# Attention with a capacity-gated expert layer: one expert's second layer kept back until the attention's last block

## The chip, the core and the metric

The kernel runs on one core of a Trainium2 chip. The metric is the time of one execution in device microseconds (us), the median of several runs. TensorE (PE in the rows) does the matmuls, VectorE (DVE), ScalarE (ACT) and GpSimd (POOL) the elementwise work, and SyncE (SP) issues most of the DMAs. Each engine works through its own list of instructions in order.

## What is computed

Attention with capped scores over 8 batches of 12 heads, 448 positions of 64 elements; then, in each batch, the 128 rows with the highest gate score go through a two-layer expert, and the result is added to them.

```python
scores = cap * np.tanh(scale * np.matmul(q, k.transpose(0, 1, 3, 2)) / cap)
attn = np.exp(scores - np.max(scores, axis=-1, keepdims=True))
attn = attn / (np.sum(attn, axis=-1, keepdims=True) + 1e-09)
x = np.matmul(attn, v)                     # -> (8, 448, 768)
gate = np.einsum('bsd,d->bs', x, w_gate)
out = x.copy()
for b in range(B):
    top_idx = np.argpartition(-gate[b], capacity)[:capacity]   # capacity 128
    xe = x[b, top_idx]
    ye = np.maximum(xe @ w1, 0.0) @ w2      # 768 -> 1024 -> 768
    g = 1.0 / (1.0 + np.exp(-gate[b, top_idx]))
    out[b, top_idx] = x[b, top_idx] + g[:, None] * ye
```

## The kernel before

Twelve heads make three groups of four, so there are 24 "doubles" (8 batches x 3 groups), numbered 0 to 23; doubles 18 to 20 are batch 6, 21 to 23 batch 7. A double takes seven steps; a step makes one 128 x 896 tile `p` (or `pl`, for the last 64 keys of two pairs): eight score matmuls (L225) into a PSUM tile `ps`, a tanh (L241) and an exp (L242) on ACT, then four value matmuls (L262, or L258 for `pl`) into the accumulators `x` and `y`. The main loop in `fast_path` takes two steps a turn: TensorE gets the scores of block u and behind them the values of block u-1, whose exps ran meanwhile. There are 84 blocks, u = 0 to 83; in turn 84 only the last values are left, and with u = 85 the loop knows the attention to be over (`u > nblocks`).

VectorE adds the tiles `p` into `e` (L277, L279) and GpSimd adds `pl` to it (L283). `sums_mm` multiplies `e` by ones (L291) for the softmax sums: two matmuls on the `e` of the first pair, two on that of the second. The sums are copied to `sm` (L294), turned (L319) and inverted into `rec` (L322, L325). The accumulators are copied to `xT` (L270), turned (L334) and multiplied by `rec` into `xn` (L338), which is stored to `out`; L351 forms its part of the gate scores.

After a batch's third double its selection runs: the scores are turned into a row (L378, L381), ranked by comparisons (L386, L393, L405), and made a one-hot matrix `sel` (L421), which a matmul turns into row numbers and gate scores (L430; `idx` L440, `gt` L444, L445). An exp on ACT makes the gate (L448). An indirect DMA of GpSimd gathers the rows `xe` (L441); six transposes (L472) and a split into two parts on ACT (`xh`, L474) and DVE (`xl`, L475) prepare them.

The expert (`expert_gen`) has a first layer of two halves of 18 matmuls (L505), each followed by a relu into `hs` (L511) and, some turns later, by four transposes (L472) and a split into `hh` and `hl`. The second layer is two halves `hf` of 24 matmuls each (L525), in two blocks of twelve; then L532 adds the gated result to `xe`, and after the second half an indirect DMA scatters the rows (L535).

`Filler` places selection and expert between the attention's work. `select` moves every selection on; `expert` takes matmuls of the expert at the head of its list, up to `BUDGET` a turn. A generator that yields `STEP` ends the turn for the experts: those behind it wait too. `K.open` allows two selected batches at a time between L430 and the end of their experts. PSUM tiles outside the attention come from two banks, `pt` and `ph`; after the attention four more are given out (`pv`, `ps`). The order on PE, ACT, DVE and POOL is the order in which this code issues; each turn first does what the turn before had deferred, and DVE's list "dve2" comes behind the turn's own `e` and `xT`.

Of the kernel before, what the change touches and what calls it, by code (L numbers as in the profile page):

```python
# [28 lines left out]
class Bank:  # L29


    def __init__(self, pool, tag, acc, wide=False):
        self.pool, self.tag, self.acc, self.wide = pool, tag, acc, wide
        self.free, self.held = (0, 0), False
# [7 lines left out]
class Ctx:  # L42

    def __init__(self):
        self.immediate = True
        self.queues = {"act": [], "dve": [], "dve2": []}
        self.t, self.epoch = 0, 1
        self.want = False
        self.tail = False
        self.x_busy = False  # L50
        self.open = 0
        self.turns = []
# [186 lines left out]
def exp_step(tc, K, D, h, c, ps):  # L239
    p = p_tile(K, D, h, c)  # L240
    tc.nc.scalar.activation(p, ps[:, :, :K.S], AF.Tanh, scale=K.sc)  # L241
    tc.nc.scalar.activation(p, p, AF.Exp, scale=K.cap)  # L242
# [225 lines left out]
def split_part(tc, K, src, hi, lo, i0, w, M):  # L468
    nc = tc.nc
    pt = K.tile_t(500, SPLIT).rearrange("p (i m) -> p i m", m=P)  # L470
    for i in range(w):
        nc.tensor.transpose(pt[:, i, :M], src[:M, (i0 + i) * P:(i0 + i + 1) * P],  # L472
                            K.ident[:M, :M])
    K.defer("act", lambda: nc.scalar.copy(hi[:, i0:i0 + w, :M], pt[:, :w, :M]))  # L474
    K.defer("dve2", lambda: nc.vector.tensor_tensor(  # L475
        lo[:, i0:i0 + w, :M], pt[:, :w, :M], hi[:, i0:i0 + w, :M].bitcast(F32),
        op=ALU.subtract))


STEP = -1  # L480


def expert_gen(tc, K, b, M, idx, gt, xe, xh, xl):
    nc = tc.nc
    S, DM, ND, NF, F = K.S, K.DM, K.ND, K.NF, K.F
    HH = DM // 2

    hs = K.hs
    hh = K.work.tile([P, NF, P], F32R, tag="mh", name="hh", bufs=1)
    hl = K.work.tile([P, NF, P], F32R, tag="ml", name="hl", bufs=1)  # L490
    turned = {}

    def turn(hf):
        split_part(tc, K, hs, hh, hl, 4 * hf, 4, M)
        turned[hf] = K.due(SPLIT)

    def first(hf):
        fs = slice(hf * 512, hf * 512 + 512)
        while not (bank := K.hold()):
            yield STEP  # L500
        ph = bank.tile()
        ops = [(xh, "w1h", i) for i in range(ND)]
        ops += [(xh, "w1l", i) for i in range(ND)] + [(xl, "w1h", i) for i in range(ND)]
        for n, (l, r, i) in enumerate(ops):
            nc.tensor.matmul(ph[:M], lhsT=l[:, i, :M], rhs=K.wts[r][:, i, fs], start=(n == 0),  # L505
                             stop=(n == len(ops) - 1))
            K.t += 233
            yield 233
        K.release(bank)
        K.want = hf == 0  # L510
        K.defer("act", lambda: nc.scalar.activation(hs[:M, fs], ph[:M], AF.Relu))  # L511
        K.turns.append((K.due(EVAC), lambda: turn(hf)))

    def wait_turn(hf):
        if K.immediate and K.turns:
            K.turns.pop(0)[1]()
        while not K.immediate and (hf not in turned or not K.past(turned[hf])):
            yield STEP

    def second(py, hf, blk, start, stop):  # L520
        ds_ = slice(hf * HH, (hf + 1) * HH)
        ops = [(hh, "w2h", i) for i in blk] + [(hh, "w2l", i) for i in blk]
        ops += [(hl, "w2h", i) for i in blk]
        for n, (l, r, i) in enumerate(ops):
            nc.tensor.matmul(py[:M, :HH], lhsT=l[:, i, :M], rhs=K.wts[r][:, i, ds_],  # L525
                             start=(start and n == 0), stop=(stop and n == len(ops) - 1))
            K.t += 176
            yield 176

    def combine(py, hf):  # L530
        ds_ = slice(hf * HH, (hf + 1) * HH)
        nc.vector.scalar_tensor_tensor(out=xe[:M, ds_], in0=py[:M, :HH], scalar=gt[:M],  # L532
                                       in1=xe[:M, ds_], op0=ALU.mult, op1=ALU.add)
        if hf:
            nc.gpsimd.indirect_dma_start(  # L535
                out=K.out[:(b + 1) * S, :],
                out_offset=bass.IndirectOffsetOnAxis(ap=idx[:M, :1], axis=0),
                in_=xe[:M], in_offset=None)

    lo_blk, hi_blk = range(4), range(4, NF)  # L540
    yield from first(0)
    yield from first(1)
    K.x_busy = False
    yield from wait_turn(0)
    for hf in range(2):
        while not (bank := K.hold()):
            yield STEP
        py = bank.tile()
        yield from second(py, hf, lo_blk, True, False)
        if hf == 0:  # L550
            yield from wait_turn(1)
        yield from second(py, hf, hi_blk, False, True)
        K.release(bank)
        K.want = hf == 0
        K.defer("dve", lambda py=py, hf=hf: combine(py, hf))
    K.open -= 1
# [82 lines left out]
def fast_path(tc, K, first, wgen):  # L639
    ND2 = K.B * K.NG  # L640
    Ds = {0: first}
    steps = [(d, h, c) for d in range(ND2) for h, c in ORDERS[d % 2]]
    sums = []
    fill = Filler()

    def at(n):
        if not 0 <= n < len(steps):
            return None
        d, h, c = steps[n]
        return Ds[d], h, c  # L650

    def flush(*names):
        q = K.take()
        for nm in names:
            for f in q[nm]:
                f()

    def turn():
        while K.turns and K.past(K.turns[0][0]) and K.t_ready():
            K.turns.pop(0)[1]()  # L660

    Ds[1] = Double(K, 1)
    Ds[1].load_qk(tc, K, 0)
    Ds[1].load_qk(tc, K, 1)
    Ds[1].load_v(tc, K)
    warm = K.banks[1].tile()
    for _ in range(WARM):
        tc.nc.tensor.matmul(warm[:, :P], lhsT=K.ident, rhs=K.ident, start=True, stop=True)
    load_consts(tc, K)
    K.immediate = False  # L670
    nblocks = len(steps) // 2
    u = 0
    while u <= nblocks or sums or fill.busy() or any(K.queues.values()):
        if u > nblocks and not sums and not K.tail:
            K.start_tail()
        q = K.take()
        for f in q["dve"] + q["act"]:
            f()
        old = [at(2 * u - 2), at(2 * u - 1)]
        new = [at(2 * u), at(2 * u + 1)]  # L680
        ps = [qk_step(tc, K, *s) for s in new if s]
        for s in old:
            if s:
                pv_step(tc, K, *s)
        for n in range(2):
            if new[n]:
                exp_step(tc, K, *new[n], ps[n])
        for s in old:
            if s:
                e_step(tc, K, *s)  # L690
                take_x(tc, K, *s)
        for f in q["dve2"]:
            f()
        for n in (2 * u, 2 * u + 1):
            if n < len(steps):
                d, i = divmod(n, 7)
                with tc.high_priority(offset=HP):
                    if i == 0 and 0 < d < ND2 - 1:
                        Ds[d + 1].load_qk(tc, K, 1)
                    if i == 2 and d + 2 < ND2:  # L700
                        Ds[d + 2] = Double(K, d + 2)
                        Ds[d + 2].load_v(tc, K)
                    if i == 4 and d + 2 < ND2:
                        Ds[d + 2].load_qk(tc, K, 0)
        if not K.tail:
            if sums:
                D = sums.pop(0)
                fill.sel.append(double_gen(tc, K, D, sums_mm(tc, K, D), fill.exp.append))
                if K.C > P and D.grp == K.NG - 1:
                    flush("dve", "act", "dve2")  # L710
                    fill.drain(K)
                    K.immediate = False
            turn()
            fill.select()
            fill.expert(BUDGET)
            flush("dve", "act", "dve2")
            for s in old:
                if s and s[1:] == (1, 2):
                    sums.append(s[0])
            turn()  # L720
            fill.select()
            if not new[0]:
                K.t += TAIL
        else:
            end = K.t + TAIL
            fill.expert(TAIL)
            K.t = max(K.t, end)
            flush("dve", "act", "dve2")
            turn()
            fill.select()  # L730
        next(wgen, None)
        u += 1
# [84 lines left out]
```

## Time and profile before

| | |
|---|---|
| time, median of three runs | 554.97 us (554.33 to 555.19) |
| the profiled execution, its own time | 556.0 us |
| its span, first to last instruction | 554.2 us |
| PE busy | 513.5 us (93%) |
| ACT, DVE, POOL busy | 360.4, 352.2, 139.2 us |
| mean granted TensorE clock | 0.988 of full |

Times below are counted from the span's start. An engine's idle time in front of an instruction is written [idle <-releaser], the releaser being what ended it; a PE instruction's own duration holds some pipeline time, so what a group costs on PE is read from its start to the next one's start. The rows are of the one profiled execution; batch 5's second layer runs from 461.9 to 485.0 us, the attention's last exp ends at 494.33, and the last matmul at 547.9.

### The profile page before, as it was taken

To read this page: it belongs to the slowest core of one execution; us is meant where nothing else is said; L and a number is where in the kernel's file an instruction comes from. 1 tells how busy PE (TensorE), PEld (TensorE's weight loads), DVE (VectorE), ACT (ScalarE), POOL (GpSimd) and SP (SyncE) were. 2 spreads that over 40 slices of the span, in tenths; PEclk is the share of its full clock that TensorE was granted. 3 is DMA by queue.
4 is the path that set the end of the run, shared out by engine and by line. 5 is a ranking of instruction groups with operands and counts; after the bars stand their busy time and mean duration, and the time that the engine had idled before them with its cause. 6 is when DMAs were issued, how large, how long until landed. Compare 5 with 4: busy or idle time off the path is not lost.

```text
span 554.2 us, 8869 instructions
## 1 busy us (share of the span) xinstructions
PE 513.5 (93%) x3446; PEld 260.4 (47%) x3446; DVE 352.2 (64%) x775; ACT 360.4 (65%) x394; POOL 139.2 (25%) x88
## 2 busy tenths in 40 slices
PE   5889989999999999999899998999999998988994
PEld 2223323354544445444454455545454454626884
DVE  1799999757636557665865565854865644865611
ACT  4987976976667574876657775686666866560110
POOL 1565532413212130431122311231313221130000
PEclk9998999999999999999999999999999999998898
DMA  7546653423214231632232331432323412212100
GB/s 256 190 156 190 193 163 119 125 86 101 74 55 149 81 100 39 186 101 84 82 108 85 114 118 34 127 130 67 99 85 107 135 47 87 67 57 69 29 30 34
DMA packets 32034, 57.63 MB, mean 104 GB/s; under 512 B 2944, under 2 KB 25984, under 8 KB 31984
## 3 DMA queue, kind: packets, MB, share of 16 engines
q1 hardware_dynamic: 30704, 50.69, 29.6%
q0 software_dynamic: 1280, 6.29, 3.4%
q8 instruction: 29, 0.48, 0.4%
q14 instruction: 21, 0.17, 0.1%
HBM read 42.81 MB, written 14.16 MB: 103 GB/s over the span
## 4 chain that ended last, share of the span: by engine, by line
PE 69%; DVE 17%; issue 5%; ACT 3%; DMA 2%; POOL 1%; POOLq 0%; DVEq 0%; SPq 0%
PE ps L225 20%; PE ph L525 9%; PE y L262 8%; PE ph L505 8%; PE x L262 8%; DVE jk L351 4%; PE pt L334 3%; PE x L258 3%; PE pt L291 3%; DVE jk L393 2%; DVE e L277 2%; DVE e L279 2%; DVE xT L270 2%; ACT p L241 2%; PE pt L472 2%
## 5 line engine op out<-in xcount | busy, mean ns | idle before, releaser
L241 ACT ACTIVATE p<-ps,sc 128x896 f32<-128x896 f32 x144 | 143.4, 996 | 73.2 <-PE ps L225 61.2
L283 POOL TENSOR_TENSOR e<-e,pl 64x896 f32<-64x896 f32 x48 | 100.5, 2093 | 288.5 <-DVE e L279 235.1
L225 PE MATMUL ps<-q,k 64*64 64x448 f32 x1344 | 150.8, 555 | 6.3 <-DMA k<-in_k 3.5
L242 ACT ACTIVATE p<-p,capc 128x896 f32<-128x896 f32 x144 | 150.2, 1043 | 4.7
L225 PEld LDWEIGHTS ps<-q,k 64*64 64x64 f32 x1344 | 43.5, 133 | 71.0 <-issue 45.8
L262 PE MATMUL y<-p,v 128*64 128x448 f32 x288 | 64.9, 556 | 0.1
L262 PE MATMUL x<-p,v 128*64 128x448 f32 x288 | 64.9, 558 | 0.0
L277 DVE TENSOR_TENSOR e<-p 128x896 f32<-128x896 f32 x48 | 59.8, 1246 | 6.6 <-ACT p L242 6.6
L279 DVE TENSOR_TENSOR e<-e,p 128x896 f32<-128x896 f32 x48 | 53.3, 1111 | 5.4 <-ACT p L242 3.8
L351 DVE CUSTOM_DVE_ANT_0 jk<-xn,wg 112x256 bf16<-112x256 f32 x96 | 51.2, 534 | 2.9
L338 DVE TENSOR_TENSOR xn<-pt,rec 112x512 f32<-112x512 f32 x39 | 26.9, 690 | 26.8 <-PE pt L334 26.2
L241 ACT ACTIVATE pl<-ps,sc 128x896 f32<-128x896 f32 x24 | 24.1, 1003 | 29.1 <-PE ps L225 28.7
L270 DVE COPY xT<-x 128x448 f32<-128x448 f32 x24 | 15.0, 623 | 39.6 <-PE x L262 25.3
L262 PEld LDWEIGHTS x<-p,v 128*64 128x64 f32 x288 | 17.7, 138 | 43.4 <-issue 31.6
L262 PEld LDWEIGHTS y<-p,v 128*64 128x64 f32 x288 | 16.3, 135 | 44.8 <-issue 31.9
L525 PE MATMUL ph<-w2h,hh 128*128 128x384 f32 x112 | 27.6, 359 | 0.0
L242 ACT ACTIVATE pl<-pl,capc 128x896 f32<-128x896 f32 x24 | 25.0, 1042 | 0.8
L505 PE MATMUL ph<-w1l,xh 128*128 128x512 f32 x84 | 25.1, 409 | 0.0
L334 PE MATMUL pt<-ident,xT 128*112 128x128 f32 x156 | 24.4, 279 | 0.7 <-DVE rec L322 0.7
L511 ACT ACTIVATE hs<-ph 128x512 f32<-128x512 f32 x14 | 8.4, 598 | 25.5 <-PE ph L505 25.3
L525 PE MATMUL ph<-w2l,hh 128*128 128x384 f32 x112 | 24.9, 345 | 0.0
L525 PE MATMUL ph<-w2h,hl 128*128 128x384 f32 x112 | 24.9, 345 | 0.0
(143 smaller groups left out, 622.6 us busy)
## 6 DMA issues: line engine op xcount, KB each, us to landing
q<-in_q SPq DMA_DIRECT2D x48, 224.0 KB, 2.6
k<-in_k SPq DMA_DIRECT2D x48, 224.0 KB, 3.2
v<-in_v SPq DMA_DIRECT2D x24, 448.0 KB, 4.1
out<-xn SPq DMA_DIRECT2D x24, 448.0 KB, 3.7
stage<-in_moe_w SPq DMA_DIRECT2D x4, 512.0 KB, 6.0
stage<-in_moe_w SPq DMA_DIRECT2D x5, 384.0 KB, 3.3
hs<-in_moe_w SPq DMA_DIRECT2D x3, 384.0 KB, 3.0
hs<-in_moe_w SPq DMA_DIRECT2D x2, 512.0 KB, 5.5
```

The costliest lines, as they stand in the source:

```text
L225: tc.nc.tensor.matmul(ps[HALF[r], j, :K.S], lhsT=kk, rhs=qq, start=True, stop=True)
L241: tc.nc.scalar.activation(p, ps[:, :, :K.S], AF.Tanh, scale=K.sc)
L242: tc.nc.scalar.activation(p, p, AF.Exp, scale=K.cap)
L262: nc.tensor.matmul(D.acc[h][HALF[j], :K.S], lhsT=D.v[:, (h * 2 + j) * 3 + c, :], rhs=p[:, j, :], start=start, stop=stop)
L277: nc.vector.tensor_tensor(D.E[h], D.P[h, 0], D.P[h, 1], op=ALU.add)
L279: nc.vector.tensor_tensor(D.E[h], D.E[h], D.P[h, 2], op=ALU.add)
L283: nc.gpsimd.tensor_tensor(e[HALF[i]], e[HALF[i]], pl[HALF[i]], op=ALU.add)
L334: nc.tensor.transpose(px[:CP, c * P:(c + 1) * P], D.xT[pair][:, c * CP:(c + 1) * CP], K.ident)
L338: nc.vector.tensor_tensor(xn[:, :, pair * P:(pair + 1) * P].rearrange("p c (h d) -> p c h d", d=K.D), px[:CP].rearrange("p (c h d) -> p c ...
L351: nc.vector.tensor_tensor_reduce(out=jk[:, :W], in0=xn[:, c, :], in1=K.wg[:, grp * W:(grp + 1) * W], scale=1.0, scalar=0.0, op0=ALU.mult, ...
L505: nc.tensor.matmul(ph[:M], lhsT=l[:, i, :M], rhs=K.wts[r][:, i, fs], start=(n == 0), stop=(n == len(ops) - 1))
L525: nc.tensor.matmul(py[:M, :HH], lhsT=l[:, i, :M], rhs=K.wts[r][:, i, ds_], start=(start and n == 0), stop=(stop and n == len(ops) - 1))
```

## The change

A flag `K.drained` is set at the top of each turn: true once all blocks of the attention have been issued. Batch 5's expert (`b == K.B - 3`), once its first layer is out and the first half of `hs` is turned, yields `STEP` until the flag is true. Its 48 matmuls L525, two L532 and its scatter L535 so move behind the attention's last values; they stay ahead of batch 6's expert, which waits in the same list. Nothing is added or dropped.

```diff
-        self.want = False
+        self.want = self.drained = False
...
     yield from first(1)
     K.x_busy = False
     yield from wait_turn(0)
+    while b == K.B - 3 and not (K.drained or K.immediate):
+        yield STEP
     for hf in range(2):
...
     while u <= nblocks or sums or fill.busy() or any(K.queues.values()):
-        if u > nblocks and not sums and not K.tail:
+        K.drained = u > nblocks
+        if K.drained and not sums and not K.tail:
             K.start_tail()
```

TensorE where the second layer of batch 5 began, before: the sums of double 21 (L291), then the held matmuls between the attention's, beside batch 6's selection (`score`, L378).

```order
L291 MATMUL pt<-e,ones 32x448 x4
L525 MATMUL ph<-w2h,hh 128x384 x4
L525 MATMUL ph<-w2l,hh 128x384 x4
L525 MATMUL ph<-w2h,hl 128x384 x4
L472 MATMUL pt<-ident,hs 128x128 x4
L225 MATMUL ps<-q,k 64x448 x8
L258 MATMUL x<-pl,v 64x448 x2
L258 MATMUL y<-pl,v 64x448 x2
L262 MATMUL x<-p,v 64x448 x2
L378 MATMUL pt<-ident,score 112x112 x4
```

The same place on TensorE now, a block and a half long.

```order
L291 MATMUL pt<-e,ones 32x448 x4
L472 MATMUL ph<-ident,hs 128x128 x4
L225 MATMUL ps<-q,k 64x448 x8
L258 MATMUL x<-pl,v 64x448 x2
L258 MATMUL y<-pl,v 64x448 x2
L262 MATMUL x<-p,v 64x448 x2
L378 MATMUL pt<-ident,score 112x112 x4
L319 MATMUL ph<-ident,sm 112x128 x4
L225 MATMUL ps<-q,k 64x448 x8
L262 MATMUL y<-p,v 64x448 x4
L334 MATMUL pt<-ident,xT 112x128 x4
```

The L525 are gone from there, and the transposes of `hs` go to bank `ph`, so that L378 no longer takes the bank that they fill.

TensorE at the end of the attention, before: the gathered rows of batch 6 are turned ahead of the last values, and its first layer (L505) follows the sums of double 23.

```order
L472 MATMUL ph<-ident,xe 128x128 x3
L472 MATMUL pt<-ident,xe 128x128 x3
L262 MATMUL y<-p,v 64x448 x4
L291 MATMUL ph<-e,ones 32x448 x4
L319 MATMUL pt<-ident,sm 112x128 x4
L505 MATMUL ph<-w1h,xh 128x512 x6
L505 MATMUL ph<-w1l,xh 128x512
L334 MATMUL pt<-ident,xT 112x128 x4
L334 MATMUL pv_4466<-ident,xT 112x128 x4
```

And now.

```order
L262 MATMUL y<-p,v 64x448 x4
L472 MATMUL pt<-ident,xe 128x128 x3
L472 MATMUL ph<-ident,xe 128x128 x3
L291 MATMUL pt<-e,ones 32x448 x4
L334 MATMUL ph<-ident,xT 112x128 x4
L525 MATMUL ph<-w2h,hh 128x384 x4
L525 MATMUL ph<-w2l,hh 128x384 x4
L525 MATMUL ph<-w2h,hl 128x384
L319 MATMUL pt<-ident,sm 112x128 x4
L334 MATMUL pv_4435<-ident,xT 112x128 x4
L334 MATMUL pv_4440<-ident,xT 112x128 x4
L525 MATMUL ph<-w2h,hl 128x384 x3
```

The held L525 come behind L291, not ahead of it, and the transposes of `xe` have moved behind the last values. Batch 7's score transposes (L378) now stand 35 L525 further down, its L430 13 L525 and 22 L505 behind them.

VectorE at the end of the attention, before: the split of batch 6's `xe` (`xl`) stands ahead of the last additions to `e`.

```order
L270 COPY xT<-x 128x448
L475 TENSOR_TENSOR xl<-ph,xh 128x384
L475 TENSOR_TENSOR xl<-pt,xh 128x384
L277 TENSOR_TENSOR e<-p 128x896
L279 TENSOR_TENSOR e<-e,p 128x896
L270 COPY xT<-y 128x448
L294 COPY sm<-ph 128x448
```

And now.

```order
L338 TENSOR_TENSOR xn<-ph,rec 112x4x128
L277 TENSOR_TENSOR e<-p 128x896
L279 TENSOR_TENSOR e<-e,p 128x896
L270 COPY xT<-y 128x448
L475 TENSOR_TENSOR xl<-pt,xh 128x384
L475 TENSOR_TENSOR xl<-ph,xh 128x384
L294 COPY sm<-pt 128x448
```

The additions to `e` now come first, the split behind them; a product `xn` of double 22 has come ahead. On GpSimd batch 5's scatter has moved from between batch 6's gather and the last two additions L283 to between the last of them and batch 7's gather, and that gather now carries a wait for the scatter's landing.

## Rows read from the trace of the kernel before

**Rows 1.** Waits of PE, 440 to 556: total us, times, longest.

```profile
PE ph L291 <- POOL e L283: 3.8, 1, 3.8
PE pt L378 <- DVE hl L475: 1.4, 1, 1.4
PE ps L430 <- DVE sel L421: 1.3, 1, 1.3
...
PE pv L378 <- DVE score L363: 0.5, 1, 0.5
PE ph L505 <- ACT xh L474: 0.3, 1, 0.3
```

**Rows 2.** Stretches: length; busy us by engine, PEclk (granted clock), DMA share, GB/s.

```profile
10.00:40.00 30.00, 27.54 (x200) 7.92 (x192) 23.75 (x19) 29.51 (x31) 15.98 (x9) 1.00 0.55 186
...
500.00:505.00 5.00, 4.87 (x18) 2.81 (x18) 1.05 (x3) 0.00 (x0) 0.07 (x1) 0.66 0.01 3
520.00:525.00 5.00, 5.00 (x21) 5.00 (x21) 1.51 (x7) 0.20 (x1) 0.96 (x1) 0.66 0.28 79
```

**Rows 3.** Timeline of PE: start, us, what, [idle before <-releaser].

```profile
461.88 0.98 PE L525 MATMUL ph<-w2h,hh 128*128 128x384 f32 x4
464.10 0.60 PE L472 MATMUL pt<-ident,hs 128*128 128x128 f32 x4
464.63 1.74 PE L225 MATMUL ps<-q,k 64*64 64x448 f32 x16
...
485.02 1.73 PE L225 MATMUL ps<-q,k 64*64 64x448 f32 x16
488.34 0.96 PE L291 MATMUL pt<-e,ones 128*32 128x448 f32 x8
...
495.43 0.94 PE L291 MATMUL ph<-e,ones 128*32 128x448 f32 x4
500.13 1.71 PE L291 MATMUL ph<-e,ones 128*32 128x448 f32 x4 [3.75 <-POOL e L283]
```

**Rows 4.** Timeline of ACT around the last two blocks.

```profile
485.87 0.20 ACT L448 ACTIVATE gt<-gt 128x1 f32<-128x1 f32 x1 [1.27 <-DVE gt L445]
...
490.28 1.01 ACT L241 ACTIVATE p<-ps,sc 128x896 f32<-128x896 f32 x1
...
493.29 1.04 ACT L242 ACTIVATE p<-p,capc 128x896 f32<-128x896 f32 x1
```

**Rows 5.** Timeline of DVE in batch 6's selection.

```profile
470.03 0.62 DVE L381 COPY row<-pt 112x448 f32<-112x448 f32 x1 [0.74 <-PE pt L378]
472.16 0.62 DVE L532 SCALAR_TENSOR_TENSOR xe<-ph,gt,xe 128x384 f32<-128x384 f32 x1 [1.50 <-PE ph L525]
...
479.08 0.87 DVE L421 TENSOR_SCALAR sel<-iota,rank 112x128 fp32r<-112x128 f32 x4
479.86 0.68 DVE L338 TENSOR_TENSOR xn<-pt,rec 112x512 f32<-112x512 f32 x1
...
482.72 1.38 DVE L351 CUSTOM_DVE_ANT_0 jk<-xn,wg 112x256 bf16<-112x256 f32 x1
...
484.14 0.42 DVE L351 CUSTOM_DVE_ANT_0 jk<-xn,wg 112x256 bf16<-112x256 f32 x1
```

**Rows 6.** Timeline of POOL, the second-last double's and the last addition to e.

```profile
481.71 2.10 POOL L283 TENSOR_TENSOR e<-e,pl 64x896 f32<-64x896 f32 x1 [15.45 <-DVE e L279]
...
498.01 2.07 POOL L283 TENSOR_TENSOR e<-e,pl 64x896 f32<-64x896 f32 x1 [3.79 <-DVE e L279]
```

**Rows 7.** Timeline of DVE at the attention's end.

```profile
495.67 1.08 DVE L277 TENSOR_TENSOR e<-p 128x896 f32<-128x896 f32 x1
496.78 1.09 DVE L279 TENSOR_TENSOR e<-e,p 128x896 f32<-128x896 f32 x1
```

**Rows 8.** DMA issues, 470 to 556: issuing queue, count, median us to landing.

```profile
out<-xe,idx POOLq DMA_INDIRECT x3, 3.8
xe<-out,idx POOLq DMA_INDIRECT x2, 4.0
```

## The prediction

> **What bounds the kernel now.** I read the waits of TensorE first, then stretches, then the timelines around the attention's end. TensorE bounds it: nearly all of its time is work, and this change neither adds nor drops any. So the prediction is a balance of what stands between the work: idle time, and work done at a slow clock. From 461.9 us on, the waits of TensorE that the change can touch are 3.8 for the last sums on GpSimd, 1.4 for the bank that L378 takes over, 1.3 for `sel`, 0.5 for the score and 0.3 for `xh` [rows 1]: 7.3 us together. (The one left out there, on `hh`, belongs to batch 7's second layer, which stays as it is.) [...] Five us at 0.66 lose 5 x 0.34 = 1.7 us of work, twice: 3.4. **Before: 7.3 + 3.4 = 10.7 us.**
>
> **What is moved.** Batch 5's 48 L525 leave the attention. Twelve take 2.22 us from start to start (461.88 to 464.10), so all take 4 x 2.22 = 8.9 us [rows 3]. They fill time behind L291 instead; two L532 on VectorE go with them (0.62 each [rows 5]), and the scatter.
>
> **Waits that end.** The 1.4 us goes: L378 no longer takes the bank that L472 filled. The waits for the score and for `sel` (0.5 and 1.3) go: ahead of batch 7's L378 now stand 35 L525, 35 x 2.22/12 = 6.5 us, and between it and L430 another 13 and 22 L505. The 0.3 for `xh` goes, since 36 L525 (6.7 us) now separate L472 from L505. The slow stretch behind the `sel` wait goes with it.
>
> **Waits that come in the attention.** I walk from the end of L291 at 461.88. A block's scores and values take 3.3 us (485.02 to 488.34), four transposes 0.53 (464.10 to 464.63) [rows 3].
> (a) L430 against the selection. TensorE needs L472, L378, L319, two L334 (5 x 0.53) and three blocks (9.9): it is at L430 at 474.5. L378 ends after 0.53 + 3.3 + 0.53, at 466.2. On VectorE row to `sel` took from 470.03 to 479.95, 9.9 us; of this the wait of 1.5 for L525 and L532's 0.6 leave, one more `xn` (0.7) is now ahead: 8.5 [rows 5]. `sel` is ready at 474.8, L430 starts at 475.0. Idle 0.5.
> (b) Behind `sel` VectorE has four L351 (0.42 and a short read each, I take 0.5), one L279 of 1.1 [rows 7], a copy of 0.6, and `idx` and `gt`, which I put at 0.4: together 4.1, so the gate's exp L448 can start at 478.9. It stands on ACT ahead of the tanh of block 82, and ACT, whose block takes 4.05 (490.28 to 494.33 [rows 4]), would have had its scores near 476.3. So ACT stands idle, and the last exp ends at 478.9 + 0.2 + 2 x 4.1 = 487.3, not 494.33: **7.0 us earlier, of 8.9 + 1.4 freed.** TensorE's price: the sums of double 22 need L283, which starts behind that L279, at 478.0, and takes 2.1 [rows 6]. TensorE reaches L291 at 475.4 + 3.3 = 478.7, does the first half in 0.94 (the price of two matmuls alone at 495.43 [rows 3]), waits 0.5 and does the second in 0.94, where both together took 0.96: 1.4 lost. After it the second scores wait 0.3 for a tanh and the last values 0.7 for the last exp: 1.0.
>
> On (b) a row shows something to weigh: L351 at 482.72 took 1.38 where the next took 0.42, and ended 0.3 after an L283 that ended at 483.81 [rows 5, 6]. In the new order L351 comes before that L283, and I charge it as unblocked. [...] Were the 1.38 the instruction's own, the last exp would come 1 us later, and the gain be 1 us less.
>
> **Waits that change at the attention's end.**
> (c) Before, L277 started at 495.67, 1.3 after the last exp (494.33), behind the split of `xe`, although its inputs were older [rows 4, 7]. Now it runs during that exp, and L279, L283 and L291 follow: 1.1 + 0.1 + 2.1 + 0.1 = 3.4 after the last exp, at 490.7; before it was 500.13 - 494.33 = 5.8. TensorE has meanwhile half the last values (0.8) and six transposes (0.8), until 488.9. The first half of L291 now takes a bank that `xl` must free: 1.1 + 0.6 (L270) + 0.6 (priced as L532, as wide) after the exp, 489.6. Idle 0.7, and 0.1 before the second half: 0.8 in place of 3.8. The held L525 do not fill this wait: they stand behind L291.
> (d) The first L525 takes the bank of an L334, freed by L294 (a copy, 0.6 as at 470.03) and `xn` (0.7) after L291 [rows 5]; with 0.1 to pass the word, less the 0.5 of that L334: idle 0.9.
>
> **Sum.** After: 0.5 + 1.4 + 1.0 + 0.8 + 0.9 = 4.6. Gain 10.7 - 4.6 = 6.1 us. Span 554.2 - 6.1 = 548.1; the profiled execution would take 556.0 - 6.1 = 549.9. The median is 1.0 below that execution, so **549.0 us**. The bounds: each of (a) to (d) at nothing would give 10.7, but (b) and (c) rest on VectorE and GpSimd rows, and I let at most 2 us of the 4.6 go: 547. On the other side small waits that the walk does not see, up to 1.5: 550.5.
>
> **The rivals.**
> One slow stretch is left. Between 488.9 and 492.9 TensorE does two half L291 and four transposes; 1.7 us of the 4 are idle. For it: the wait for `sel`, 1.3 us, was enough before 520. Against it: the 1.4 us at 468 was followed by no slow clock, and 10 to 40 us, an attention without the expert, has 1.00 [rows 2]. Price 1.7: 550.7. [...]
>
> VectorE and the gate hold the attention; this is the slower case. VectorE is the engine with little room there, and ACT may not start a block before L448. Each us that `gt` comes after 478.9 moves the last exp by a us. If it stays at the old 485.87 [rows 4], the last exp stays at 494.3, and behind it come 8.9 us more of L525; saved there are 3.8 + 0.5 + 1.3 + 0.3 + 3.4 = 9.3, less (c) and (d), 1.7: 8.9 - 9.3 + 1.7 = 1.3 us slower, 556.3. It decides when the last exp gains less than 1.3 us, which needs `gt` 5.7 us later than in my walk. Against it: of VectorE's time from row to `sel`, 2.1 us leave by reading.
>
> The gather of batch 7 now waits on GpSimd for batch 5's scatter. The scatter can be issued some 9 us (48 L525) behind the first L525, and lands 3.8 later; L430 comes 22 L505 behind it, then the gather, 4.0 [rows 8]. An L505 is no shorter than an L525, so 22 are 4.1 or more: it is close. If the gather is late by 1 us the time is 550; the 36 L525 and the last L472 follow it, with no other work to take. It would have to be 6 us late to undo the change. I give it 2 us: 551.
>
> The flag does not hold: by the order of instructions it does, and I leave it 0.01, which stands with "between" below.
>
> **How the numbers follow.** Forecast 549.0: 0.52. A slow stretch left (550.7): 0.22. The gather late (551): 0.07. Half of the attention's gain lost to the gate (552.5): 0.06. The gate in full or other waits of that size: 0.07 at 556, and 0.06 between, where the sum comes to nothing. Two runs of this kernel can be told apart by 0.2%, 1.1 us: faster 0.87, same 0.06, slower 0.07. The range reaches from the lower bound, 547.0, to the gate's half case, 552.5.
>
> **What would show it.** Right: the last exp near 487, ACT idle some 2.5 us before L448, L291's last half within 4 us of the last exp, no wait at batch 7's L378, L430 and L472, granted clock 1.00 after the first L525. Wrong: `sel` of batch 6 later than 476, a clock of 0.66 around 493, or an idle TensorE ahead of the last L472 of `xe`. If the last exp moves by less than 1.3 us, the sign of my forecast is wrong.

## The result, and the profile after

The changed kernel takes **548.37 us** (median of five runs, 547.77 to 549.35) beside 554.97 us (554.33 to 555.85) for the kernel before in the same comparison: a ratio of **0.988, with a 95% interval of 0.987 to 0.990**, 6.6 us faster. The forecast was 549.0 us, with a range of 547.0 to 552.5. The profiled execution of the changed kernel took 547.77 us, its span is 546.0 us, the mean granted clock 0.998 (before: 556.0, 554.2 and 0.988).

The two profiled executions are already 1.0 us apart when the changed part begins: the sums of double 21 (the L291 just ahead of batch 5's second layer) start at 460.99 us before and at 459.95 after. From there to the end of the last L525 it was 86.9 us (460.99 to 547.90) and is now 79.95 (459.95 to 539.90): **7.0 us less in the part that the change touches**. This stretch is the measure of every trace below.

First the waits of TensorE in the changed kernel from 440 us to the end (columns: engine, tile and line that waited, what for, total us, times, longest).

```profile
PE pt L291 <- DVE xl L475: 1.0, 1, 1.0
PE ph L525 <- DVE xn L338: 0.8, 1, 0.8
PE ph L291 <- POOL e L283: 0.5, 1, 0.5
PE ph L525 <- ACT hh L474: 0.5, 1, 0.5
PE y L262 <- ACT p L242: 0.5, 1, 0.5
PE pt L291 <- POOL e L283: 0.2, 1, 0.2
```

Of the five waits of [rows 1] four are gone; of the first, at the last sums, 0.2 is left (the last row here), beside a new 1.0 for `xl`. The one on `hh` was there before too (0.7) and stands for batch 7's second layer; the other four are new.

The stretches of the changed kernel at and behind the attention's end (busy us by engine, granted clock, DMA share, GB/s), which answer to [rows 2]:

```profile
489.00:494.00 5.00, 4.04 (x24) 2.68 (x23) 2.97 (x10) 0.00 (x0) 0.46 (x1) 1.00 0.19 51
494.00:499.00 5.00, 5.00 (x34) 5.00 (x32) 4.28 (x15) 0.00 (x0) 0.00 (x0) 1.00 0.46 132
```

The granted clock is 1.00 in these and in every other five us from 484 to 529: neither of the two stretches at 0.66 is left.

TensorE from `sel` to the first held L525, the timeline that answers to [rows 3] (start, us, what, [idle before <-releaser]):

```profile
473.36 0.76 PE L430 MATMUL pt<-vals,sel 112*128 112x4 f32 x4
...
477.36 0.95 PE L291 MATMUL ph<-e,ones 128*32 128x448 f32 x4
478.84 0.95 PE L291 MATMUL ph<-e,ones 128*32 128x448 f32 x4 [0.53 <-POOL e L283]
479.72 1.82 PE L225 MATMUL ps<-q,k 64*64 64x448 f32 x16
...
485.56 0.97 PE L262 MATMUL y<-p,v 128*64 128x448 f32 x4 [0.46 <-ACT p L242]
...
488.39 0.95 PE L291 MATMUL pt<-e,ones 128*32 128x448 f32 x4 [1.05 <-DVE xl L475]
489.51 0.95 PE L291 MATMUL pt<-e,ones 128*32 128x448 f32 x4 [0.18 <-POOL e L283]
...
491.82 0.98 PE L525 MATMUL ph<-w2h,hh 128*128 128x384 f32 x4 [0.78 <-DVE xn L338]
```

In place of the 3.75 us at L291 stand 1.05 and 0.18, and L430 has no idle time ahead of it.

ACT around the gate and the last exp, which answers to [rows 4]:

```profile
477.43 0.20 ACT L448 ACTIVATE gt<-gt 128x1 f32<-128x1 f32 x1 [2.23 <-DVE gt L445]
...
484.47 1.04 ACT L242 ACTIVATE p<-p,capc 128x896 f32<-128x896 f32 x1
```

The last exp ends at 485.51, where it ended at 494.33: 8.8 us earlier, 7.8 of them from the changed part. The gate still makes ACT stand idle, now for 2.2 us.

VectorE and GpSimd in the same stretch, which answer to [rows 5 to 7]:

```profile
465.44 0.61 DVE L381 COPY row<-pt 112x448 f32<-112x448 f32 x1
...
472.92 0.87 DVE L421 TENSOR_SCALAR sel<-iota,rank 112x128 fp32r<-112x128 f32 x4
473.70 0.42 DVE L351 CUSTOM_DVE_ANT_0 jk<-xn,wg 112x256 bf16<-112x256 f32 x1
...
477.94 1.80 DVE L277 TENSOR_TENSOR e<-p 128x896 f32<-128x896 f32 x1
...
484.36 0.69 DVE L338 TENSOR_TENSOR xn<-ph,rec 112x512 f32<-112x512 f32 x1
484.96 1.08 DVE L277 TENSOR_TENSOR e<-p 128x896 f32<-128x896 f32 x1
486.15 1.09 DVE L279 TENSOR_TENSOR e<-e,p 128x896 f32<-128x896 f32 x1
487.16 0.62 DVE L270 COPY xT<-y 128x448 f32<-128x448 f32 x1
487.69 0.55 DVE L475 TENSOR_TENSOR xl<-pt,xh 128x384 fp32r<-128x384 f32 x1
```

```profile
476.71 2.08 POOL L283 TENSOR_TENSOR e<-e,pl 64x896 f32<-64x896 f32 x1 [10.41 <-PE x L262]
...
487.38 2.08 POOL L283 TENSOR_TENSOR e<-e,pl 64x896 f32<-64x896 f32 x1 [4.25 <-PE ph L472]
506.24 1.01 POOL L535 DMA_INDIRECT out<-xe,idx  x1 [16.77 <-DVE sel L421]
```

From the row to the end of `sel` it is 8.35 us (465.44 to 473.79), where it was 9.9; the last L279 ends 1.7 us after the last exp, where it ended 3.5 after it.

### The profile page after: what moved, and what is told of

Its sections match the earlier page's. It is cut to its first block, busy times and chain, and to the rows that moved or that the text cites. A ratio compares the mean times of both kernels' runs of the same rounds, so it can differ in the third digit from the quotient of the medians.

```text
span 546.0 us, 8868 instructions
## 1 busy us (share of the span) xinstructions
PE 511.2 (94%) x3446; PEld 258.0 (47%) x3446; DVE 351.8 (64%) x775; ACT 360.2 (66%) x394; POOL 140.6 (26%) x88
## 4 chain that ended last, share of the span: by engine, by line
PE 66%; DVE 21%; issue 6%; ACT 3%; DMA 2%; POOL 1%; DVEq 0%; POOLq 0%; ACTq 0%
PE ps L225 18%; PE ph L525 9%; PE ph L505 8%; PE y L262 8%; PE x L262 6%; DVE jk L351 3%; PE pt L334 3%; DVE e L277 3%; PE x L258 3%; PE pt L291 2%; DVE xT L270 2%; DVE jk L393 2%; DVE e L279 2%; DVE w1l L177 2%; PE pt L472 2%
## 5 line engine op out<-in xcount | busy, mean ns | idle before, releaser
L283 POOL TENSOR_TENSOR e<-e,pl 64x896 f32<-64x896 f32 x48 | 100.5, 2094 | 283.4 <-DVE e L279 216.8
L277 DVE TENSOR_TENSOR e<-p 128x896 f32<-128x896 f32 x48 | 60.6, 1262 | 6.6 <-ACT p L242 6.6
L279 DVE TENSOR_TENSOR e<-e,p 128x896 f32<-128x896 f32 x48 | 53.3, 1111 | 5.3 <-ACT p L242 3.5
L351 DVE CUSTOM_DVE_ANT_0 jk<-xn,wg 112x256 bf16<-112x256 f32 x96 | 50.3, 524 | 2.9
L338 DVE TENSOR_TENSOR xn<-pt,rec 112x512 f32<-112x512 f32 x37 | 25.5, 690 | 24.8 <-PE pt L334 24.2
L535 POOL DMA_INDIRECT out<-xe,idx x8 | 8.2, 1021 | 74.3 <-DVE xe L532 48.8
L525 PE MATMUL ph<-w2h,hh 128*128 128x384 f32 x104 | 25.4, 358 | 1.3 <-DVE xn L338 0.8
L291 PE MATMUL pt<-e,ones 128*32 128x448 f32 x176 | 23.9, 551 | 2.3 <-POOL e L283 1.3
L294 DVE COPY sm<-pt 128x448 f32<-128x448 f32 x22 | 13.7, 621 | 18.6 <-PE pt L291 18.6
L475 DVE TENSOR_TENSOR hl<-pt,hh 128x512 fp32r<-128x512 f32 x13 | 8.9, 688 | 25.1 <-ACT hh L474 25.0
L334 PE MATMUL pt<-ident,xT 128*112 128x128 f32 x148 | 23.2, 279 | 0.8 <-DVE rec L322 0.8
```

Of the source, the lines that this page charges most:

```text
L277: nc.vector.tensor_tensor(D.E[h], D.P[h, 0], D.P[h, 1], op=ALU.add)
L279: nc.vector.tensor_tensor(D.E[h], D.E[h], D.P[h, 2], op=ALU.add)
L283: nc.gpsimd.tensor_tensor(e[HALF[i]], e[HALF[i]], pl[HALF[i]], op=ALU.add)
L291: nc.tensor.matmul(ps[32 * i:32 * i + 32, :S], lhsT=K.ones, rhs=D.E[i // 2][:, i % 2, :], start=True, stop=True)
L334: nc.tensor.transpose(px[:CP, c * P:(c + 1) * P], D.xT[pair][:, c * CP:(c + 1) * CP], K.ident)
L351: nc.vector.tensor_tensor_reduce(out=jk[:, :W], in0=xn[:, c, :], in1=K.wg[:, grp * W:(grp + 1) * W], scale=1.0, scalar=0.0, op0=ALU.mult, ...
```

## The experiments

The theory: the gain is waits and slow clock, in two places. Inside the attention the selection no longer stands in TensorE's way; at the attention's end the split of batch 6's `xe` has moved behind the last additions to `e`, so that the last sums come earlier. The rivals: the gain is one of the two alone, or it is limited by the gate on ACT. Of the eight kernels, two begin at the kernel before and six at the changed one. Line numbers shift by a few in some (L295 there is L291 here).

**The late split alone.** The kernel before, with only batch 6's `xe` transposes and split kept back until the last values have been issued; batch 5's second layer stays in the attention.

```diff
-        self.want = False
+        self.want = self.last = False
...
         yield from K.wait(8000)
+        while b == K.B - 2 and not (K.last or K.immediate):
+            yield
...
     while u <= nblocks or sums or fill.busy() or any(K.queues.values()):
+        K.last = u >= nblocks
```

> The kernel before, with one thing of the change done alone: batch 6's transposes and split of xe wait until the attention's last values have been issued. Batch 5's second layer stays in the attention. Theory (the gain is a sum of waits at several places): the chain from the last exp to the second half of the last L291 shrinks from 5.8 to about 3.4 us as in the changed kernel, but the waits for L378's bank (1.4), for the score (0.5) and for sel (1.3) stay, and at least one of the two slow stretches with them; new waits for xl and xn cost about 1. 1 to 4 us faster, 551 to 554. Rival (the order at the attention's end is all that matters; where batch 5's matmuls stand is indifferent): nearly the full 6.6 us, 548 to 549.5.

Measured: 550.57 us, 0.992 (0.990 to 0.993) of the kernel before, a gain of 4.1 us: a little faster than the theory's 551 to 554, and short of the rival's 548 to 549.5. With the split gone from its old place, the planner puts double 22's L319, a first L334 and an `xn` there, as in the changed kernel. Its waits of TensorE:

```profile
PE ph L291 <- DVE xl L477: 1.6, 1, 1.6
PE pt L378 <- DVE hl L477: 1.4, 1, 1.4
PE ph L430 <- DVE sel L421: 1.2, 1, 1.2
...
PE ph L507 <- ACT xh L476: 0.3, 1, 0.3
PE ph L291 <- POOL e L283: 0.2, 1, 0.2
```

The waits of the selection stay (1.4 and 1.2), and only the one of the last sums has shrunk, from 3.8 to 1.8. In the trace the stretch is 82.6 us, 4.3 less: 2.6 in waits (7.3 to 4.7, the score's 0.5 went too) and 1.7 for one slow stretch. The one that is left follows the wait of 1.6; behind the `sel` wait the clock was 1.00 here.

```profile
499.00:504.00 5.00, 5.00 (x22) 3.30 (x19) 3.11 (x11) 0.00 (x0) 0.00 (x0) 0.66 0.18 50
...
519.00:524.00 5.00, 5.00 (x32) 4.83 (x30) 1.13 (x2) 0.14 (x1) 0.07 (x1) 1.00 0.28 79
```

So the larger part of the change's 6.6 us can be had without moving a single L525 of batch 5.

**The idle time filled.** The kernel before, with 14 matmuls of 128 x 512 ahead of the last sums; nothing reads their result.

```diff
+            if u > nblocks and sums:
+                warm = K.banks[0].tile()
+                for _ in range(14):
+                    tc.nc.tensor.matmul(warm, lhsT=K.wts["w1h"][:, 0, :P], rhs=K.wts["w1h"][:, 0, :512],
+                                        start=True, stop=True)
             D = sums.pop(0)
```

> The kernel before, with 14 more matmuls (128x512, of weights, whose result nobody reads) between the last values and the last sums, where TensorE waits 3.75 us; they take about 3.3 us of it and end before the sums can start. Theory (slow clock is a cost of its own, 1.7 us a stretch): granted clock 1.00 from 500 to 505, the last L291 back to about 0.95 us from 1.71, and 1.5 to 1.8 us faster, 553.3. Rival (behind the sums VectorE's score chain is the bound, and a slow TensorE there costs nothing): within 0.5 us of before, with a longer wait at L378.

Measured: 553.19 us, 0.998 (0.997 to 0.999), 1.4 us faster, as the theory had it (553.3). TensorE does 3.5 us of work for nobody in the time in which it had waited, and what comes behind runs faster:

```profile
494.74 3.49 PE L709 MATMUL pt<-w1h 128*128 128x512 f32 x14 [0.45 <-DVE xl L475]
498.16 1.89 PE L291 MATMUL ph<-e,ones 128*32 128x448 f32 x8
```

```profile
499.00:504.00 5.00, 4.76 (x31) 3.34 (x29) 1.78 (x5) 0.00 (x0) 0.06 (x1) 1.00 0.00 0
```

Where [rows 2] had 0.66 there is 1.00. The idle time before the last sums thus cost its 3.75 us and, behind it, a slow stretch on top, worth 1.4 us in the medians (1.7 by the trace of before).

**The gate later.** The changed kernel, with batch 6's gate (L448 and its two VectorE steps) issued behind the split of `xe`, so that it no longer stands ahead of a tanh.

```diff
-        K.defer("dve2", gate)
+        if b != K.B - 2:
+            K.defer("dve2", gate)
...
+        if b == K.B - 2:
+            K.defer("dve2", gate)
```

> The changed kernel, with batch 6's gate (the exp L448 and two small operations behind it) moved from the middle of the last blocks to behind the attention, where its expert starts; it is needed only by L532 much later. Theory (the 2.2 us for which ACT stands idle before L448 reach TensorE only as the 0.5 us that its last values wait for the last exp, since the score, sum and transposing work is on TensorE anyway): ACT's idle time gone, 0.3 to 0.8 us faster than the changed kernel, 547.6 to 548.1. Rival (ACT sets the attention's end, as my walk in the prediction has it): 2 us faster than the changed kernel, 546.4.

Measured: 548.39 us, 0.989 (0.987 to 0.990): no faster than the changed kernel. Beside its own runs of the kernel before it gains 6.2 us (the changed kernel 6.6), and the measured stretch is 79.90 us (79.95). Both expectations fell, the theory's 0.3 to 0.8 and the rival's 2. ACT and TensorE in it:

```profile
481.69 1.01 ACT L241 ACTIVATE p<-ps,sc 128x896 f32<-128x896 f32 x1 [1.51 <-PE ps L225]
```

```profile
489.20 0.94 PE L291 MATMUL pt<-e,ones 128*32 128x448 f32 x4 [1.63 <-DVE xl L478]
```

ACT no longer waits for the gate; it waits for TensorE's scores instead. The wait of the last values is gone (0.46), but the one of the last sums has risen from 1.05 to 1.63. What ends it is a chain on VectorE that the last exp has no part in: in the changed kernel's rows above, `xn` of double 22 (484.36), L277 and L279, the copy `xT` (487.16) and `xl` (487.69) follow each other with gaps of 0.1 us at most, and `xn` waits for double 22's sums on TensorE. Counted from double 21's L291, the last exp now ends 0.67 us earlier, but L279 starts only 0.09 earlier. An earlier exp only waits longer for that chain. The wait of 1.63 is the one that was followed by 0.66 in the first experiment; here the clock stayed at 1.00 behind it:

```profile
489.00:494.00 5.00, 3.84 (x20) 2.10 (x21) 3.27 (x12) 0.00 (x0) 1.26 (x1) 1.00 0.03 9
494.00:499.00 5.00, 5.00 (x35) 4.96 (x34) 4.18 (x17) 0.00 (x0) 0.00 (x0) 1.00 0.49 137
```

**Half of the layer held.** The changed kernel, with the first 24 of batch 5's L525 back in the attention and only the second half kept back.

```diff
-    while b == K.B - 3 and not (K.drained or K.immediate):
-        yield STEP
     for hf in range(2):
+        while hf and b == K.B - 3 and not (K.drained or K.immediate):
+            K.want = False
+            yield STEP
```

> The kernel before, with only the second half (24 of 48 matmuls) of batch 5's second layer held until the attention is over. Theory (what counts is which waits end, not how many matmuls move): the split of batch 6 still comes behind the last additions, the waits for the score and sel and both slow stretches still end, the 1.4 us at L378 stays, and the gate still holds ACT by some 3 us; about 5 us faster, 549.5 to 550.5. Rival (the gain goes with the work moved): half of 6.6, 551.7.

Measured: 549.69 us, 0.991 (0.989 to 0.992), where the theory had 549.5 to 550.5. Its only wait of the selection is the 1.4 us for the bank (L378), the last sums have 1.0 and 0.2, and its granted clock is 1.00 from 484 to 529. Half of the layer brings 4.9 of the 6.6 us.

**The split early again.** The changed kernel, with batch 6's split of `xe` due earlier, so that it stands ahead of the last values and of the last additions to `e`, as in the kernel before; the 48 L525 stay behind the attention.

```diff
-        yield from K.wait(8000)
+        yield from K.wait(5000 if b == K.B - 2 else 8000)
```

> The changed kernel, with batch 6's transposes and split of xe put back ahead of the last values and the last additions to e, where they stood before (a shorter allowance for its gather). All 48 matmuls of batch 5 still come behind the attention. Theory (two separate parts: the order at the attention's end gave some 2.5 us and with it mostly one slow stretch, the matter behind it the rest): the last sums wait for GpSimd about 3.5 us again, and the run is 2 to 4 us slower than the changed kernel, 550.5 to 552.5. Rival (the held matmuls alone make the gain): 548.4, as the changed kernel.

Measured: 553.79 us, 0.998 (0.997 to 0.999) of the kernel before: a gain of 1.1 us, 5.5 short of the changed kernel's 6.6, and worse than the expected 550.5 to 552.5. VectorE at the split, TensorE, and the stretches around it:

```profile
486.82 0.56 DVE L475 TENSOR_TENSOR xl<-pt,xh 128x384 fp32r<-128x384 f32 x1 [2.94 <-ACT xh L474]
...
487.76 1.08 DVE L277 TENSOR_TENSOR e<-p 128x896 f32<-128x896 f32 x1
```

```profile
487.52 0.95 PE L291 MATMUL pt<-e,ones 128*32 128x448 f32 x4
492.22 1.71 PE L291 MATMUL pt<-e,ones 128*32 128x448 f32 x4 [3.75 <-POOL e L283]
493.86 1.10 PE L319 MATMUL ph<-ident,sm 128*112 128x128 f32 x4
495.23 1.65 PE L525 MATMUL ph<-w2h,hh 128*128 128x384 f32 x4 [0.27 <-DVE rec L322]
496.67 1.16 PE L525 MATMUL ph<-w2l,hh 128*128 128x384 f32 x4
497.67 0.34 PE L525 MATMUL ph<-w2h,hl 128*128 128x384 f32 x1
```

```profile
489.00:494.00 5.00, 1.78 (x5) 0.33 (x6) 1.53 (x3) 0.00 (x0) 2.07 (x1) 0.65 0.00 0
494.00:499.00 5.00, 4.73 (x24) 4.28 (x25) 1.55 (x4) 0.00 (x0) 0.00 (x0) 0.67 0.00 0
```

VectorE stands idle 2.94 us ahead of the split, for `xh`, which ACT makes only behind the last exp; the additions L277 and L279, and GpSimd's L283 behind them, must wait for the split. (In the kernel before VectorE stood idle 2.33 us there, for the same.) The 3.75 us at the last sums are back to the hundredth, and the slow clock with them. By trace it is 85.15 us against 79.95, 5.2 more: 2.5 are idle time at the last sums (3.75 against 1.23), and some 2.4 are the work behind them, done at the lower clock: the second half of L291 takes 1.64 from start to start (492.22 to 493.86) where it took 0.88, the four L319 1.1 where 0.44, the first eight L525 1.44 and 1.00 where 0.71 each at the full clock. The other waits come to nearly the same. Only the split's due time was edited; the planner with it put double 22's L319, L334 and `xn` back behind the last sums, where the kernel before has them. The wait for `xh` shows that it is the split that holds the additions up.

The four kernels make a table of gains, each beside the runs of the kernel before in its own comparison (medians of 554.63 to 554.97):

| us gained | 48 L525 in the attention | 48 L525 held |
|---|---|---|
| split ahead of the last additions | 0 (before) | 1.1 |
| split behind them | 4.1 | 6.6 (after) |

The split's place is worth 4.1 us in one column and 5.5 in the other, holding the layer 1.1 in one row and 2.5 in the other. The diff does not speak of the split at all: that order comes out of the planner, whose count of time (`K.t`, 176 for each L525) runs differently when TensorE's turns lack the 48 L525. The split is due 8000 of this count behind the gather (`K.wait(8000)`), and this experiment, with 5000, puts it back.

**Banks earlier, and the held matmuls ahead of the sums.** What is left in the changed kernel at the attention's end are waits for a bank and an order in which the held work stands behind the waiting L291. First three of the attention's PSUM banks are given out one turn earlier, nothing else:

```diff
-        self.banks += [Bank(self.psV[i], f"V{i}", True) for i in range(2)]
+        self.banks.append(Bank(self.psV[1], "V1", True))
+        self.banks[-1].free = (self.t, 0)
+
+    def early_banks(self):
+        self.banks.append(Bank(self.psV[0], "V0", True))
         self.banks += [Bank(self.psS, "S", False, True) for i in range(2)]
...
+        if u == nblocks:
+            K.early_banks()
```

> The changed kernel, with three of the four PSUM banks of the attention that are given out after it (one accumulator, two for scores) given out one turn earlier, when the last scores are out. The transposes of xe then take other banks than the last sums. Theory: the wait of the first half of the last L291 for xl (1.05) and that of the first L525 for xn (0.78) end, the second half waits about 0.9 for GpSimd instead of 0.2; 1.0 us faster than the changed kernel, 547.3. Rival (these waits stand beside VectorE's score chain, which then sets batch 7): no gain, 548.4, with a wait at batch 7's L378 or L430 instead.

Measured: 547.60 us, 0.986 (0.984 to 0.988), near the theory's 547.3; the measured stretch is 78.95 us, 1.0 less. The 1.05 for `xl` is gone, 0.9 for the addition itself has come, and the first L525 no longer waits; of the rival's wait at batch 7's L378 there is 0.2. Then, on top of it, the flag is set one turn earlier, so that 15 of the held L525 come ahead of the last sums:

```diff
-        K.drained = u > nblocks
+        K.drained = u >= nblocks
         if u == nblocks:
             K.early_banks()
-        if K.drained and not sums and not K.tail:
+        if u > nblocks and not sums and not K.tail:
```

> As the run with the earlier banks, and the held matmuls let go one turn earlier too: 15 of them (2.7 us) then stand ahead of the last sums, in the wait that the change leaves unfilled. Theory (the balance of waits on TensorE is the time): no idle time ahead of the last sums or the first L525, 2.0 us faster than the changed kernel, 546.4; sel of batch 7 comes 1 us later but still before TensorE gets there. Rival (the selection of batch 7 becomes the bound, as it hangs on these sums): no faster than with the banks alone, and a new wait at batch 7's L378, L430 or L472 of 1 us or more.

Measured: 546.10 us, 0.984 (0.982 to 0.986), 1.5 less than the banks alone, where the theory had 546.4:

```profile
488.30 0.95 PE L529 MATMUL ph<-w2h,hh 128*128 128x384 f32 x4
...
491.12 0.96 PE L295 MATMUL pt<-e,ones 128*32 128x448 f32 x8
```

No row here has idle time, and the eight L295 stand together at 0.96. Last, the later gate on top of that:

> As the run with the held matmuls ahead of the last sums, and with batch 6's gate moved behind the attention. Theory: the gate alone gave nothing because a wait for xl took its place; with that wait gone the 0.5 us of the last values for the last exp should now count: 0.3 to 0.6 us faster than without it, 545.9. Rival (VectorE's chain from xn over the last additions sets the last sums, not ACT): same as without it.

Measured: 545.51 us, 0.983 (0.981 to 0.985), the fastest of all: 9.4 us below the kernel before, where the changed kernel is 6.6 below it. The step from 546.10 is 0.6 us, as expected; the 0.46 that the last values waited for their exp are gone from its waits, and the measured stretch is 76.77 us after 77.43. But 0.6 us is 0.1% and the intervals overlap, so the medians alone do not show it.

## Why the prediction was right, and where it was not

**Total and sign: right**, by 0.6 us. The balance of what stands between TensorE's work was the right account. It foresaw 10.7 - 4.6 = 6.1; by the rows of after it is 10.7 - 3.9 = 6.8 (the 3.9 being 1.47 and 0.46 of (b), 1.23 of (c) and 0.78 of (d)), and the two stretches differ by 7.0; the wait on `hh`, which the sum left out, is 0.2 shorter.

**The waits that were to end: right, all of them**, those for the bank, the score, `sel` and `xh`, and, in the trace, the two slow stretches.

**(a) L430 against the selection: 0.5 expected, 0 measured.** The selection took 8.35 us where 8.5 was worked out, and TensorE came 12.5 us behind the end of L291 (460.85 to 473.36) where 12.6 was. L430 started 0.4 us before the last piece of `sel` was done, and nothing waited. That fits four L430 that need four pieces of `sel` one after the other; the sum had charged all four pieces to the first.

**(b) The gate and the sums of double 22: the price right, its cause half wrong.** The split sums cost 2.36 us (477.36 to 479.72) where an undivided L291 costs 0.89: 1.47, foretold 1.4. The last values waited 0.46 where 1.0 was taken for them and the second scores together. The last exp came 7.8 us earlier, foretold 7.0. But the bold step that carried this part, that the gate on ACT sets the attention's end, is what the later gate refuted: taking it away gained nothing, since the last sums hang on VectorE's chain behind `xn`. Only where other work covers the last sums (the last experiment, beside the one before it) do the traces show the 0.46 as gained.

On the reading of L351: it took 0.42 in the new order, where 1.38 had stood, with no GpSimd addition beside it, so charging it as unblocked was right. In the changed kernel it is L277 that meets one: it took 1.80 in place of 1.08, while L283 ran from 476.71 to 478.79, and 478.79 + 1.08 = 479.87 is within 0.15 us of its end (479.74). In the kernel with the later gate L277 was issued 0.6 us earlier, counted back from the second half of L291 that this L283 releases (478.21 to 479.74, in the changed kernel 477.94 to 478.84); it took 2.42 and ended no earlier: at 480.63, 0.9 us behind that L291's start in both.

**(c) The last sums: 0.8 expected, 1.23 measured** (1.05 and 0.18), in place of 3.75. The walk took `xl` to end 2.3 us after the last exp; the first half of L291 started 2.9 after it (485.51 to 488.39), since L279 began not at the last exp's end but at 486.15, behind `xn` and L277. Those two, at the end of the chain from double 22's sums, were missing from the walk. The step was right where it mattered: 3.75 - 1.23 = 2.5 us is the largest single gain of the sum, and with the slow stretch behind it (1.7) it is 4.2 of the 7.0. What the prediction did not say is that this part hangs on the order that the planner chose, and can be had without taking one matmul out of the attention, as the table shows.

**(d) The first L525: 0.9 expected, 0.78 measured.**

**The slow stretches: counted too surely.** The prediction charged both stretches of one trace (0.66 from 500 to 505 us, behind the last sums, and from 520 to 525, behind the `sel` wait that ends at 519.25) as fixed parts of the kernel before; their price, 5 x 0.34 each, is an estimate from the 0.66 of [rows 2]. The one behind the last sums came with their 3.75 us in both kernels that have them, and went where this time was filled. The one behind the `sel` wait does not always come: with the same wait (1.19 us in the late split alone, 1.29 with the idle time filled) the two experiments made from the kernel before have a clock of 1.00 there. The clock over all runs does speak for about two stretches less: it is 0.991 in the median of the 34 runs of the kernel before that stood beside the experiments, and 0.997 in that of the changed kernel's five (0.994 to 0.999); 0.006 of 550 us are 3.3 us, and 3.4 were charged. Where in those runs the stretches lay, and whether the changed kernel's runs at 0.994 and 0.995 have one at the attention's end, no trace here shows.

**From the profiled execution to the median.** The prediction took the profiled execution to be 1.0 us above the median, before and after alike, and so expected 549.9 us for it; it was 547.77, below its median. The kernel before had in its profiled run one slow stretch more, early in the attention (its clock from 40 to 50 us), that the changed one's run did not have (1.00 there). Its clock, 0.988, is the lowest that the kernel before showed. So it is in part luck that a sum made from this one trace met the medians within 0.6 us. The rows of the early stretch:

```profile
40.00:45.00 5.00, 3.00 (x14) 0.98 (x16) 4.79 (x9) 2.06 (x3) 3.55 (x3) 0.78 0.85 273
45.00:50.00 5.00, 5.00 (x40) 1.45 (x36) 4.97 (x9) 3.23 (x5) 0.38 (x1) 0.88 0.65 205
```

**The rivals.** A slow stretch left (550.7): not in the trace, where the clock stayed at 1.00 through the waits of 1.05, 0.18 and 0.78, and through the attention's end without batch 5's second layer (1.00 from 459.95 to 489.00). The rival was not far, though: the late split alone had the slow stretch behind 1.63 us of idle time (0.66 from 499 to 504), the kernel with the later gate had none behind the same 1.63 (1.00 from 489 to 499). The gate and VectorE (556.3): no, `gt` came in time. The gather of batch 7: nearly. Batch 5's scatter was issued at 506.24 (the row above), 14.4 us behind the first L525 where some 9 were taken, and the wait for its landing stands on VectorE, ahead of the gather: `idx`, ready to be written behind an L430 of 507.24, had to wait for it:

```profile
509.42 0.16 DVE L440 TENSOR_SCALAR idx<-ps 128x1 int32<-128x1 f32 x1 [2.86 <-DMA out<-xe,idx]
```

The mechanism is there, but TensorE had L505 and L525 to do meanwhile, and its L472 of `xe` (from 514.14) show no idle time.

## What to carry to other kernels

When a filler is moved, compare the order of everything that the same planner places, and price the reordered step by itself: here a split of which the diff says nothing was worth 4.1 to 5.5 us, the 48 matmuls that it names 1.1 to 2.5. Follow the chain that ends a wait back over all engines before paying for its nearest member: an ACT stall of 2.2 us could be taken away for nothing gained, because VectorE's queue ended the wait. And look where the moved work lands: the same matmuls, put 15 ahead of the waiting sums instead of behind them, with banks free to take them, gave another 1.5 us.

## What the runs showed of the hardware

Executions of the same kernel differ in TensorE's mean granted clock. The 34 runs of the kernel before that stood beside the experiments have from 0.988 to 0.994; the four at 0.988 took 555.5 us in the mean, the eight at 0.994 took 553.9. The clocks differ by 0.006 of 554 us, 3.3 us, as much as two five-us stretches at 0.66 lose; the times differ by 1.6 us, half of that. So not every such stretch costs the kernel its 1.7 us; which do, these means cannot tell.

In single us of the kernel before the clock is 1.00 ahead of its slow stretches and behind them, and 0.50 at the lowest within them (0.58, 0.50, 0.50, 0.71 from 500 to 504; 0.82, 0.50, 0.50, 0.50, 0.97 from 520 to 525). With TensorE's wait of 3.75 us a stretch whose mean lies between the two came in both kernels that have this wait (0.66 in the kernel before, and 0.65 and 0.67 in two stretches of five us with the split early again); behind 1.63 us it came in one kernel (0.66, the late split alone) and not in another (1.00, the later gate), behind 1.19 to 1.29 us in one of three (0.66 in the kernel before; 1.00 in the two made from it), behind the 1.4 us at batch 6's L378 in none of the four kernels that have it (the twelve L525 next to it take 2.20 us from start to start in each). What decides in the shorter cases stays open.
